# A new pass that orders the queues of a fused attention and gated feed-forward kernel

## The chip, the cores and the metric

The kernel runs on one core of a Trainium2 chip. The core has a matrix engine (TensorE, PE in the rows; its weight loads are PEld), a vector engine (VectorE, DVE), a scalar engine (ScalarE, ACT), a third vector engine (GpSimd, POOL) and a queue that issues transfers (SyncE, SP). The metric is the time of one execution on the device in microseconds (us); smaller is better.

## The reference

The inputs are `q`, `k`, `v` of 8 batches, 8 heads, 576 positions and 64 columns, and three weights. A sliding window of 64 positions bounds the attention, and a gated feed-forward part with a convolution over three neighbouring positions follows:

```python
scores = q @ k^T / 8, kept where 0 <= query - key < 64
attn = softmax(scores)
x = (attn @ v) with the heads side by side          # 8 x 576 x 512
h = maximum(x @ w_in, 0)                            # 8 x 576 x 1024
conv_out = sum of conv_w[k] * h shifted by k - 1    # k = 0, 1, 2
gate = 1 / (1 + exp(-conv_out))
return (h * gate) @ w_out                           # 8 x 576 x 512
```

The weights come to the kernel as words of 64 bits and are turned into 32-bit numbers on the chip.

## The kernel before, in words

The 4608 positions (8 x 576) are cut into NU = 12 units of 384. A unit passes through these steps; the names are those of the functions.

- `qk` (line 330): the scores of one of four parts ("b") of a unit, in two PSUM banks `sc`; in unit 0 two parts use banks `po` instead. `row_max` (337, DVE) adds the mask and takes the largest score of a row, `exps` (347, ACT) the exponentials, `guard` (350), `reciprocal` (353) and `normalise` (358) the division, on DVE in units 0 to 2 and on GpSimd later. In units 0 and 1 `transpose_pe` (364) turns the result round on PE and `untile` (369) copies it to `ub`; later `transpose` (374, DVE) and `place` (386, transfers) do that.
- `values` (441): attention times `v` for one of four groups of columns, in one of two banks `acc`; `split_hi` (445, ACT) and `split_lo` (448, DVE) write it as a high part `xh` and a low part `xl`.
- `mm1` (461): for each of eight blocks f of 128 hidden columns, twelve matmuls in two halves of six, `xh` by `wih`, `xh` by `wil`, `xl` by `wih`, in the same two banks `acc`; `relu` (478, 482) brings the block to `hbuf`. `conv_mid` (488, ACT), `conv_side` (495, DVE, two passes), `sig` (502), `gate` (507), `gate_hi` (511) and `gate_lo` (515) make `gh` and `gl`.
- `mm2` (524): twelve matmuls for each f into four banks `po`, copied to `ot` (555 by ACT, 557 by DVE) and written out (559, 561).

`weights` and `to_f32` (231 to 256) bring in one or two blocks of weights: the transfer (249) lands in `bits`, ACT takes an absolute value (233), GpSimd a maximum (234), DVE shifts (235), joins (237) and adds (241), ACT scales the low words (240), GpSimd casts to the high part (254), DVE subtracts to the low part (255). While this goes on, during the first units, PE fills idle time with matmuls that nobody reads (`keep_busy`, 201), written "fills" below.

What sets the order: every step is put down with `at(t, engine, cost, ...)`: a planned time `t` in units of one block f, an engine, a cost in us, and what it reads and writes. The function `queued` walks through the steps with a clock of its own. For each engine it knows when that engine is free (`free`) and which steps are ready; it takes the one that can start first, and among the ready ones of that engine the smallest `t`. The order in which it takes them is the order of the instructions in each engine's queue; nothing is reordered later. Where the pass sees PE idle between 2 and 110 us of its own clock, it puts in 4 fills per us. The planned times of the lead-in (unit 0, unit 1, weights) and of the later units stand in the table START. PE's costs count 1.75 times before WARM = 34 us of the pass's clock:

```python
end = free[e] = start + turn + x.cost * (1.75 if e == "PE" and start < WARM else 1.0)
```

A group of a unit's steps stands in one call: `moe(u)` puts down `mm1`, `mm2` and what belongs to them, `attend(u + 1, ...)` the values of the next unit, `softmax(u + 2, ...)` the scores of the one after.

Of the kernel before, what the change touches and what calls it, by code (L numbers as in the profile page):

```python
# [8 lines left out]
F32 = mybir.dt.float32  # L9
# [20 lines left out]
BY_PE = 2  # L30
MASKED = -8.0e9
# [17 lines left out]
class Work:  # L49


    def __init__(self, t, eng, cost, do, r, w, kind, mb):
        self.t, self.eng, self.cost, self.do, self.r, self.w, self.kind, self.mb = t, eng, cost, do, r, w, kind, mb
        self.needs, self.after, self.ready = 0, [], 0.0


def queued(works, fill=None):
# [25 lines left out]
    done = 0.0  # L83
# [4 lines left out]
    dma, order, left, now = 0.0, [], len(works), 0.0  # L88
    while left:
        best = None  # L90
        for e, ws in waiting.items():
# [3 lines left out]
            if best is None or start < best[0]:  # L95
# [3 lines left out]
                key=lambda x: x.t - (0.5 if x.kind and x.kind == state[e] else 0.0))  # L99
        waiting[e].remove(x)  # L100
        if fill and e == "PE" and start < FILL_TO:
            t = max(done, FILL_FROM)
            n = int((start - t) * FILL)

            clean = [(end, k) for k, (by, end) in touched.items() if by != "PE" and end < t]
            if n > 0 and clean:
                order.append(Work(x.t, e, 0.0, fill(n, min(clean)[1]), [], [], None, 0))
        if e == "PE":
            done = start + x.cost
# [22 lines left out]
    "v0": -27.718,  # L132
    "pv0": -16.652,
    "conv": -50.105,
    "bits": ((-54.407, -55.57), (-39.376, -39.449)),
    "qk1": -30.664,
    "v1": -7.347,
    "qk2": -0.865,
    "qk0": (-89.392, -49.783, -60.199, -45.186),
    "ex0": (-41.041, -35.906, -29.408, -23.745),  # L140
    "sc1": (-28.59, -27.038, -11.919, -7.749),
    "ex1": (-7.86, -0.101, 0.495, 2.41),
    "mask": -0.464,
    "sig": ((3.579, 6.501, 8.86, 9.928), (2.077, 5.642, 5.863, 10.537), (3.828, 7.108, 8.794, 11.179)),
    "in": (-33.296, -27.752, -22.771, -21.836, -16.12),
    "out": (-13.132, -6.394, 4.658, 7.697),
    "pv": ((4.523, 1.038, 6.096, 5.282), (5.491, 6.42, 7.385, 7.606), (2.552, 5.391, 5.803, 6.224)),
    "ex": ((7.752, 8.302, 8.53, 10.388), (7.962, 8.724, 10.881, 11.654), (5.306, 6.637, 8.454, 9.014)),
}
SWITCH = {"PE": 0.12, "ACT": 1.28}  # L150
WARM = 34.0
# [4 lines left out]
def attention_moe(ctx: ExitStack, tc: tile.TileContext, q, k, v, w_in, conv_w, w_out, out):  # L156
# [50 lines left out]
    def at(t, eng, cost, do, r=(), w=(), kind=None, mb=0):  # L207
        plan.append(Work(t, eng, cost, do, list(r), list(w), kind, mb))


    def load_qk(t, u):

        cut = (0, NX // 2 + W, NX + W), (0, NX // 2, NX)
        for g in range(2):
# [14 lines left out]
    def to_f32(t, n, st, x, kb, kt):  # L229
# [4 lines left out]
        at(t, "POOL", 0.0026 * n + 0.5, lambda: nc.gpsimd.tensor_scalar(x, x, TINY, None, op0=ALU.max), w=kt)  # L234
        at(t, "DVE", 0.00052 * n + 0.25, lambda: nc.vector.tensor_scalar(  # L235
            xu, xu, 3, 0x3FFFFFF8, op0=ALU.logical_shift_left, op1=ALU.bitwise_and), w=kt)
        at(t, "DVE", 0.00104 * n + 0.1, lambda: nc.vector.scalar_tensor_tensor(  # L237
# [3 lines left out]
        at(t, "DVE", 0.00104 * n + 0.1, lambda: nc.vector.tensor_tensor(xu, xu, lw, ALU.add), r=kb, w=kt)  # L241

    def weights(t, src, fs, hi, lo, key, buf, halves):
# [10 lines left out]
        at(t, "POOL", 0.0014 * n + 0.25, lambda: nc.gpsimd.tensor_copy(hi, x), r=kt, w=[f"{key}{f}h" for f in fs])  # L254
        at(t, "DVE", 0.00104 * n + 0.1, lambda: nc.vector.tensor_tensor(lo, x, hi.bitcast(F32), ALU.subtract),  # L255
# [132 lines left out]
    def softmax(u, qk_at, ex_at):  # L388
        for b in range(4):
            g, t = b // 2, qk_at[b]  # L390
            at(t, "PE", 0.70 if wide(u) else 0.62, lambda b=b: qk(u, b), r=[("q", g, b % 2)] + [("k", g, i) for i in range(b % 2 + 1)], w=bank_keys(u, b) + [("turn", b)],
               kind="tiled" if wide(u) else "eight")
            for i in range(NB):
                if block(u, b, i)[1]:
                    at(t + 0.1, "POOL", 0.2, lambda b=b, i=i: nc.gpsimd.memset(ss[b][:, i, :, :W], 0.0), w=[("s", b, i)])
            at(t + 0.17, "DVE", 1.27 if wide(u) else 1.1, lambda b=b: row_max(u, b),
               r=bank_keys(u, b) + (["mask0"] if wide(u) else ["mask1", "mask2"]), w=[("s", b, i) for i in range(NB)] + [("nm", b)])
            t = ex_at[b]
            for i in range(NB):
                at(t, "ACT", 0.78 if wide(u) else 0.74, lambda b=b, i=i: exps(u, b, i), r=[("nm", b)],  # L400
                   w=[("s", b, i), ("sm", b, i)], kind="exp")
            t += 0.45
            sw = [("sm", b, i) for i in range(NB)]
            if u < 3:
                at(t, "POOL", 0.6, lambda b=b: guard(b, nc.gpsimd), w=sw)
            else:
                at(t, "DVE", 0.15, lambda b=b: guard(b, nc.vector), w=sw)
            at(t, "DVE", 0.15, lambda b=b: reciprocal(b), r=sw, w=[("r", b)])
            if u < 3:
# [10 lines left out]
            else:  # L420
                t = max(t, when[-1][2] + 0.1)
                at(t, "DVE", 0.72, lambda b=b: transpose(b), r=sr, w=[("T", g)] + [("bits", i, a) for i in T_BITS[g] for a in range(2)])
                if b % 2:
                    if u == BY_PE:
                        at(t + 0.01, "POOL", 1.0, lambda g=g: zero_blocks(g), w=[("u", g, i) for i in range(4)])
# [161 lines left out]
    for u in range(NU):  # L587
# [5 lines left out]
        for c in range(NC):  # L593
            attend(u + 1, c, pv[c])
# [89 lines left out]
```

## Time and profile before

| | before |
|---|---|
| time, median of 3 runs | 534.14 us (533.28 to 535.07) |
| the profiled execution | 533.38 us |
| its span in the profile | 531.6 us |
| PE busy / weight loads | 523.1 us (98%) / 499.2 us |
| DVE / ACT / GpSimd busy | 381.1 / 405.5 / 115.9 us |
| clock granted to PE | 0.998 of full speed |
| chain that ended last | PE 88%, DVE 10%, ACT 1% |

Busy PE time holds the fills too, so it does not say how much of it is wanted work. A timeline row gives the start, the length and the form of one instruction, or of several alike in a row ("x24"). Matmuls overlap in it: the next one starts before the one before has ended, so the pace of PE is read from start to start. A matmul of `qk`, `values` or a fill is two matrix instructions in the trace (an order that says x12 is x24 there).

### The profile page before, as it was taken

The page shows a single profiled execution, that of the slowest core. Times are in us where ns is not written, and L with a number is a line of the kernel's source. Part 1 is how long each engine was busy: PE and PEld are TensorE (multiplying, and loading weights), DVE is VectorE, ACT ScalarE, POOL GpSimd, SP SyncE. Part 2 cuts the span into 40 slices and gives each one's busy share as a digit, 9 for nine tenths or more (in the row PEclk, how much of TensorE's full clock was granted, in tenths as well). Part 3 has the DMA queues.
Part 4 walks back from the last instruction along what each step waited for, and adds up shares of the span by engine and source line. Part 5 has one row for each costly group of instructions (what it writes and reads, how often), then busy time and mean ns, then how long its engine had stood idle before and what let it go on. Part 6 is the DMA issues. An engine that isn't in the chain of part 4 may idle for free.

```text
span 531.6 us, 14870 instructions
## 1 busy us (share of the span) xinstructions
PE 523.1 (98%) x5802; PEld 499.2 (94%) x5802; DVE 381.1 (72%) x1108; ACT 405.5 (76%) x1034; POOL 115.9 (22%) x208
## 2 busy tenths in 40 slices
PE   9999999999999999999999999999999999999996
PEld 8888889999999999999999999999999999999996
DVE  4899999986677677676686776776776865864552
ACT  5889886799888788689689679779769769653541
POOL 6556663203121121112012022022022011100000
PEclk9999999999999999999999999999999999999999
DMA  8883760166472282273173164254155133110011
GB/s 286 318 300 123 263 224 20 27 181 211 125 249 55 76 252 65 76 236 85 48 241 106 42 222 132 47 198 156 46 185 170 46 121 105 46 61 0 1 60 61
DMA packets 29318, 69.98 MB, mean 132 GB/s; under 512 B 5696, under 2 KB 17472, under 8 KB 29248
## 3 DMA queue, kind: packets, MB, share of 16 engines
q1 hardware_dynamic: 29248, 69.03, 40.5%
q8 instruction: 46, 0.75, 0.6%
q14 instruction: 24, 0.20, 0.1%
HBM read 47.73 MB, written 9.47 MB: 108 GB/s over the span
## 4 chain that ended last, share of the span: by engine, by line
PE 88%; DVE 10%; ACT 1%; issue 1%; POOL 0%
PE po L524 38%; PE acc L461 35%; PE acc L441 6%; PE sc L330 6%; PE acc L201 2%; DVE w L241 1%; DVE c L495 1%; DVE s L337 1%; DVE w L237 1%; DVE wil L255 1%; DVE s L358 1%; DVE w L235 1%; DVE xl L448 1%; ACT ub L369 0%; ACT s L347 0%
## 5 line engine op out<-in xcount | busy, mean ns | idle before, releaser
L524 PE MATMUL po<-gh,woh 128*128 128x386 f32 (+1 forms) x384 | 133.1, 347 | 0.0
L461 PE MATMUL acc<-xh,wih 128*128 128x384 f32 x384 | 131.9, 344 | 1.1 <-DVE xl L448 0.9
L461 PE MATMUL acc<-xh,wil 128*128 128x384 f32 x384 | 129.8, 338 | 0.4 <-DVE wil L255 0.4
L524 PE MATMUL po<-gl,woh 128*128 128x386 f32 (+1 forms) x384 | 130.1, 339 | 0.0
L461 PE MATMUL acc<-xl,wih 128*128 128x384 f32 x384 | 129.7, 338 | 0.0
L524 PE MATMUL po<-gh,wol 128*128 128x386 f32 (+1 forms) x384 | 129.7, 338 | 0.0
L495 DVE SCALAR_TENSOR_TENSOR c<-hbuf,cw,c 128x386 f32<-128x386 f32 (+1 forms) x192 | 110.8, 628 | 19.9 <-ACT c L488 19.0
L347 ACT ACTIVATE s<-s,nm 128x96 f32<-128x96 f32 (+2 forms) x288 | 105.6, 371 | 9.7 <-DVE nm L337 9.3
L358 POOL TENSOR_TENSOR s<-s,r 128x576 f32<-128x576 f32 x36 | 45.7, 1271 | 196.4 <-DVE r L353 196.4
L524 PEld LDWEIGHTS po<-gh,woh 128*128 128x128 f32 x384 | 72.3, 188 | 4.3
L461 PEld LDWEIGHTS acc<-xh,wih 128*128 128x128 f32 x384 | 72.1, 188 | 4.2 <-DVE xl L448 1.6
L461 PEld LDWEIGHTS acc<-xh,wil 128*128 128x128 f32 x384 | 72.2, 188 | 0.7 <-DVE wil L255 0.7
L524 PEld LDWEIGHTS po<-gl,woh 128*128 128x128 f32 x384 | 72.4, 188 | 0.0
L524 PEld LDWEIGHTS po<-gh,wol 128*128 128x128 f32 x384 | 72.4, 188 | 0.0
L461 PEld LDWEIGHTS acc<-xl,wih 128*128 128x128 f32 x384 | 72.1, 188 | 0.0
L337 DVE CUSTOM_DVE_ANT_0 s<-sc,mask 128x96 f32<-128x96 f32 (+2 forms) x276 | 53.2, 254 | 21.3 <-PE sc L330 20.5
L515 DVE TENSOR_TENSOR gl<-c,gh 128x772 fp32r<-128x772 f32 (+1 forms) x48 | 52.8, 1099 | 20.1 <-ACT gh L511 19.5
L502 ACT ACTIVATE c<-c 128x772 f32<-128x772 f32 (+1 forms) x48 | 40.8, 850 | 33.8 <-DVE c L495 33.5
L482 ACT ACTIVATE hbuf<-acc 128x384 f32<-128x384 f32 x64 | 30.6, 487 | 34.7 <-PE acc L461 34.1
L347 ACT ACTIVATION_READ_ACCUMULATOR s<-s,nm 128x1 f32 x288 | 55.1, 191 | 0.0
L488 ACT ACTIVATE c<-hbuf,cw 128x386 f32<-128x386 f32 (+1 forms) x96 | 53.7, 610 | 0.1
L507 DVE TENSOR_TENSOR c<-c,hbuf 128x772 f32<-128x772 f32 (+1 forms) x48 | 45.2, 942 | 9.2 <-ACT c L502 9.2
(64 smaller groups left out, 641.8 us busy)
## 6 DMA issues: line engine op xcount, KB each, us to landing
v<-in_v_dram SPq DMA_DIRECT2D x24, 768.0 KB, 4.7
ub<-T SPq DMA_DIRECT2D x240, 48.0 KB, 2.0
k<-in_k_dram SPq DMA_DIRECT2D x22, 448.0 KB, 5.3
q<-in_q_dram SPq DMA_DIRECT2D x22, 384.0 KB, 6.2
out_dram<-T SPq DMA_DIRECT2D x8, 772.0 KB, 3.5
T<-in_w_in_dram SPq DMA_DIRECT2D x8, 512.0 KB, 5.4
T<-in_w_out_dram SPq DMA_DIRECT2D x8, 512.0 KB, 4.3
out_dram<-T SPq DMA_DIRECT2D x3, 768.0 KB, 6.1
```

Source lines behind the costliest of these rows:

```text
L330: nc.tensor.matmul(banks_of(u, b)[h][r:r + rows, i * P + o:i * P + n], qs[hs, 2 * g + p, t:t + rows], ks[hs, 2 * g + p, t + o:t + n], star ...
L337: nc.vector.tensor_tensor_reduce(out=ss[b][:, i, h, o:n], in0=banks_of(u, b)[h][:, i * P + o:i * P + n], in1=mask[m][:, o:n], scale=-0.125 ...
L347: nc.scalar.activation(x, x, AF.Exp, bias=nms[b][:, e], scale=-1.0, accum_out=sms[b][:, e])
L358: on.tensor_tensor(sv, sv, rs[b].unsqueeze(2).broadcast_to([P, 2 * NB, n]), ALU.mult)
L441: nc.tensor.matmul(acc[bank(("v", u, c))][h * D:(h + 1) * D, t * W:(t + 1) * W], vs[:, c, t, h], ub[g][:, 2 * p:2 * p + 2, 2 * t + h], sta ...
L461: nc.tensor.matmul(acc[bank(("m", u, f))][:, :NX], w[:, f, c], x[u % 2][:, c], start=(c == 0 and j == 0), stop=(c == NC - 1 and j == 2))
L488: nc.scalar.activation(cs[i % 2][:, a, :n], hbuf[:, f, 1:1 + n], AF.Copy, scale=cw[:, 1, f:f + 1])
L495: nc.vector.scalar_tensor_tensor(c, hbuf[:, f, e:e + n], cw[:, e, f:f + 1], c, op0=ALU.mult, op1=ALU.add)
L502: nc.scalar.activation(c, c, AF.Sigmoid)
L507: nc.vector.tensor_tensor(c, c, hbuf[:, 2 * i:2 * i + 2, 1:1 + n], ALU.mult)
L515: nc.vector.tensor_tensor(gls[ring(u, i)][:, :, :n], cs[i % 2][:, :, :n], ghs[ring(u, i)][:, :, :n].bitcast(F32), ALU.subtract)
L524: nc.tensor.matmul(po[o][:, :n], w[:, f, es], x, start=(f == 0 and j == 0), stop=(f == NF - 1 and j == 2))
```

## The change

- The pass `queued` gets a sixth argument of a step, `port`: how long it holds what DVE and GpSimd cannot use at once. A step of DVE that has it starts no earlier than the last such step of GpSimd ends in the pass's clock, and the other way round. `two(...)` puts down a step that holds it for its whole cost (tensor operations on DVE with operands in SBUF, the cast and the normalisation on GpSimd); GpSimd's maximum holds it for PORT_CL = 0.5 us only.
- Several costs are set anew (line by line in the diff), WARM goes from 34 to 5, and the whole table START is new. Among it: the first two weight transfers change places, and the times of `values`, `exps` and `sig` in the later units move.
- The scores of part n of unit u + 2 are put down beside the values of column group n, by `scores`, one part at a time; the load of `q` and `k` follows after every second part.
- The copy of the last bank of the last unit is cut in two halves of 193 columns, one on ACT and one on DVE, each with its own transfer.
- LATE, CATCH and CAST_ACT and the argument `early` stand at values with which they change nothing.

```diff
+        if x.port:
+            if e == "POOL" and start < port["DVE"]:
+                free[e] = port["DVE"]
+                continue
+            start = max(start, port["POOL"])
+            port[e] = start + x.port
...
-            t = max(done, FILL_FROM)
+            t = max(free[e], FILL_FROM)
...
-    "bits": ((-54.407, -55.57), (-39.376, -39.449)),
+    "bits": ((-51.706, -50.713), (-31.489, -48.442)),
...
-    "pv": ((4.523, 1.038, 6.096, 5.282), (5.491, 6.42, 7.385, 7.606), (2.552, 5.391, 5.803, 6.224)),
+    "pv": ((4.247, 1.621, 6.62, 5.614), (4.827, 3.03, 5.128, 5.557), (4.971, 4.767, 5.829, 5.368)),
...
-WARM = 34.0
+PORT_CL = 0.5
+WARM = 5.0
...
-        at(t, "POOL", 0.0026 * n + 0.5, lambda: nc.gpsimd.tensor_scalar(x, x, TINY, None, op0=ALU.max), w=kt)
+            at(t, "POOL", 0.0027 * n + 0.02, lambda: nc.gpsimd.tensor_scalar(x, x, TINY, None, op0=ALU.max), w=kt, port=PORT_CL)
...
+            if u == LAST and o == NC - 1:
+                for eng, cost, cut, copy in (("ACT", 0.3, slice(0, w // 2), nc.scalar.copy), ("DVE", 0.3, slice(w // 2, w), nc.vector.tensor_copy)):
+                    at(t + 0.05 * o, eng, cost, lambda cut=cut, copy=copy: copy(ot[:, NC - 1, cut], po[NC - 1][:, cut]), r=[("po", o)], w=[("ot", o, cut.start)])
+                    at(t + 0.05 * o + 0.01, "SP", 0.7, lambda cut=cut: nc.sync.dma_start(out[u, :, NC - 1, cut], ot[:, NC - 1, cut]), r=[("ot", o, cut.start)], mb=0.1)
+                continue
...
+    coming = [(u, b) for u in range(2, NU) for b in range(4)]
...
+        for n, (x, y) in enumerate(zip(pv, START["ex"][min(u, 2)])):
+            if u > 0 or n >= LATE:
+                scores(x + 0.005, n0 + y, n)
```

The numbers of all instructions of each kind stay as they are, but for 102 fills in the place of 93, the extra half copy, its transfer, and 42 loads of ACT's function tables in the place of 58.

Two places show how the queues move. The first is PE's queue in a later unit (values of two groups, then scores; `acc_110` and `acc_111` are the two banks, `ub_61` and `ub_62` the two halves of a unit's attention, 12 matmuls a group, 24 to a part of the scores, all but the first two of which are left out). Before:

```order
1409 L441 MATMUL acc_111<-ub_61,v 64x64 x12
1410 L441 MATMUL acc_110<-ub_62,v 64x64 x12
1411 L330 MATMUL sc_108<-k,q 32x96
1412 L330 MATMUL sc_109<-k,q 32x96
...
1485 L461 MATMUL acc_111<-xl_65,wih 128x384
1486 L441 MATMUL acc_110<-ub_62,v 64x64 x12
1487 L330 MATMUL sc_108<-k,q 32x96
1488 L330 MATMUL sc_109<-k,q 32x96
...
1511 L524 MATMUL po_113<-gh_99,woh 128x386
```

And now:

```order
1404 L479 MATMUL acc_111<-xl_65,wih 128x384
1405 L349 MATMUL sc_108<-k,q 32x96
1406 L349 MATMUL sc_109<-k,q 32x96
...
1429 L459 MATMUL acc_110<-ub_62,v 64x64 x12
1430 L459 MATMUL acc_111<-ub_62,v 64x64 x12
1431 L349 MATMUL sc_108<-k,q 32x96
1432 L349 MATMUL sc_109<-k,q 32x96
...
1455 L542 MATMUL po_113<-gh_99,woh 128x386
```

The four groups of values of a unit stood in three places, one pair and two alone; now they stand in two pairs, the second of them directly between two parts of scores.

The second place is the start of ACT's queue (`s_80` to `s_82` are parts 0 to 2 of unit 0's scores, `w_105` the first two blocks of `w_in`). Before:

```order
2 L347 ACTIVATE s_80,sm_88<-s_80,nm_84 128x64 x2
3 L347 ACTIVATE s_80,sm_88<-s_80,nm_84 128x128 x4
4 L347 ACTIVATE s_81,sm_89<-s_81,nm_85 128x128 x6
5 L233 ACTIVATE w_105<-T 128x512
6 L347 ACTIVATE s_82,sm_90<-s_82,nm_86 128x64 x2
```

And now:

```order
2 L366 ACTIVATE s_80,sm_88<-s_80,nm_84 128x64 x2
3 L366 ACTIVATE s_80,sm_88<-s_80,nm_84 128x128 x2
4 L246 ACTIVATE w_105<-T 128x512
5 L366 ACTIVATE s_80,sm_88<-s_80,nm_84 128x128 x2
6 L246 ACTIVATE w_105<-T 128x512
7 L366 ACTIVATE s_81,sm_89<-s_81,nm_85 128x128 x6
```

The first block of weights now stands ahead of the last exponentials of part 0, and the second ahead of those of part 1.

## Rows read from the trace of the kernel before

**Rows 1.** Windows: length, busy us (instructions) of PE, PEld, DVE, ACT, POOL; clock; DMA

```profile
0.00:34.47 34.47, 32.51 (x433) 29.39 (x433) 24.57 (x100) 25.96 (x96) 22.06 (x62) 1.00 0.87 308
34.47:75.13 40.66, 38.26 (x496) 34.95 (x497) 40.62 (x115) 35.11 (x97) 22.78 (x18) 1.00 0.59 195
110.00:527.44 417.44, 417.44 (x4552) 401.07 (x4550) 280.66 (x825) 318.22 (x794) 58.79 (x112) 1.00 0.37 115
```

**Rows 2.** The same view of the fills alone (line 201): length, PE, PEld

```profile
0.00:34.47 34.47, 22.20 (x138) 19.27 (x138) 1.00 0.87 308
34.47:75.13 40.66, 4.68 (x38) 4.66 (x38) 1.00 0.59 195
```

**Rows 3.** Waits of PE, whole span: us in total, times, longest

```profile
PE acc L441 <- DVE xl L448: 1.1, 1, 1.1
...
PE acc L461 <- DVE xl L448: 0.9, 2, 0.5
PE acc L441 <- DMA v<-in_v_dram: 0.8, 1, 0.8
PE acc L461 <- DVE wil L255: 0.4, 1, 0.4
PE acc L461 <- POOL w L234: 0.2, 1, 0.2
```

**Rows 4.** Timeline of PE in a later unit: start, length, instruction

```profile
347.77 1.62 PE L441 MATMUL acc<-ub,v 128*64 128x64 f32 x48
349.32 0.83 PE L330 MATMUL sc<-k,q 64*32 64x96 f32 x48
...
355.76 0.34 PE L461 MATMUL acc<-xl,wih 128*128 128x384 f32 x1
356.02 0.92 PE L441 MATMUL acc<-ub,v 128*64 128x64 f32 x24
356.87 0.83 PE L330 MATMUL sc<-k,q 64*32 64x96 f32 x48
357.64 0.45 PE L524 MATMUL po<-gh,woh 128*128 128x386 f32 x1
357.92 0.34 PE L524 MATMUL po<-gh,wol 128*128 128x386 f32 x1
```

**Rows 5.** Chain that ended last: the last run of matmuls

```profile
514.79 12.66 PE po L524 x72
```

**Rows 6.** Timeline of PE: eight fills and the matmul behind them

```profile
39.68 1.93 PE L201 MATMUL po<-spare 128*128 128x112 f32 x16
41.59 0.42 PE L461 MATMUL acc<-xh,wih 128*128 128x384 f32 x1
```

**Rows 7.** Timelines of GpSimd and DVE: operations that overlap

```profile
40.10 2.78 POOL L234 TENSOR_SCALAR w<-w 128x1024 f32<-128x1024 f32 x1 [2.21 <-ACT w L233]
...
40.28 1.67 DVE L358 TENSOR_TENSOR s<-s,r 128x768 f32<-128x768 f32 x1
41.87 1.21 DVE L241 CUSTOM_DVE_ANT_0 w<-T,w 128x2048 uint16<-128x2048 uint16 x1
```

**Rows 8.** Lead-in: transfer issued at 4.80 (us to landing), ACT, DVE

```profile
T<-in_w_in_dram SPq DMA_DIRECT2D x1, 512.0 KB, 6.0
...
8.82 0.38 ACT L347 ACTIVATE s<-s,nm 128x128 f32<-128x128 f32 x1
...
12.86 0.96 DVE L358 TENSOR_TENSOR s<-s,r 128x768 f32<-128x768 f32 x1
```

**Rows 9.** Timeline of DVE in a later unit: conv_side pair, end of a row_max

```profile
351.24 1.15 DVE L495 SCALAR_TENSOR_TENSOR c<-hbuf,cw,c 128x386 f32<-128x386 f32 x2
...
358.82 0.08 DVE L337 DVE_READ_ACCUMULATOR2_ANT nm<- 128x1 f32 x1
```

**Rows 10.** The end: DVE's last copy, the last four transfers on SP

```profile
527.47 0.56 DVE L557 COPY T<-po 128x386 f32<-128x386 f32 x1 [0.49 <-PE po L524]
...
526.41 1.98 SPq L559 DMA_DIRECT2D out_dram<-T  x4
```

More of the change, by code (lines that the diff above doesn't have):

```diff
@@ L30 @@
 BY_PE = 2
+LATE = 0
+CATCH = 99
+CAST_ACT = 99
 MASKED = -8.0e9
@@ L87, in queued @@
             waiting[x.eng].append(x)
-    dma, order, left, now = 0.0, [], len(works), 0.0
+    dma, port, order, left = 0.0, {"DVE": 0.0, "POOL": 0.0}, [], len(works)
     while left:
@@ L106, in queued @@
             if n > 0 and clean:
-                order.append(Work(x.t, e, 0.0, fill(n, min(clean)[1]), [], [], None, 0))
-        if e == "PE":
-            done = start + x.cost
+                order.append(Work(x.t, e, 0.0, fill(n, min(clean)[1]), [], [], None, 0, 0.0))
         turn = SWITCH[e] if e in SWITCH and (x.kind != state[e] if e == "PE" else x.kind and x.kind != state[e]) else 0.0
@@ L205, in attention_moe, with at, two, load_qk @@
     plan = []
-    def at(t, eng, cost, do, r=(), w=(), kind=None, mb=0):
-        plan.append(Work(t, eng, cost, do, list(r), list(w), kind, mb))
-    def load_qk(t, u):
+    def at(t, eng, cost, do, r=(), w=(), kind=None, mb=0, port=0.0):
+        plan.append(Work(t, eng, cost, do, list(r), list(w), kind, mb, port))
+    def two(t, eng, cost, do, **kw):
+        at(t, eng, cost, do, port=cost, **kw)
+    def load_qk(t, u, gs=(0, 1)):
         cut = (0, NX // 2 + W, NX + W), (0, NX // 2, NX)
-        for g in range(2):
+        for g in gs:
             c = slice(2 * g, 2 * g + 2)
@@ L253, in weights @@
         to_f32(t, n, st, x, kb, kt)
-        at(t, "POOL", 0.0014 * n + 0.25, lambda: nc.gpsimd.tensor_copy(hi, x), r=kt, w=[f"{key}{f}h" for f in fs])
-        at(t, "DVE", 0.00104 * n + 0.1, lambda: nc.vector.tensor_tensor(lo, x, hi.bitcast(F32), ALU.subtract),
+        if key == "out" and fs[0] >= CAST_ACT:
+            at(t, "ACT", 0.0009 * n + 0.2, lambda: nc.scalar.copy(hi, x), r=kt, w=[f"{key}{f}h" for f in fs])
+        else:
+            two(t, "POOL", 0.00127 * n, lambda: nc.gpsimd.tensor_copy(hi, x), r=kt, w=[f"{key}{f}h" for f in fs])
+        two(t, "DVE", 0.00104 * n + 0.07, lambda: nc.vector.tensor_tensor(lo, x, hi.bitcast(F32), ALU.subtract),
            r=kt + [f"{key}{f}h" for f in fs], w=[f"{key}{f}l" for f in fs])
@@ L584, in attention_moe, with scores @@
     load_v(START["v1"], 1)
-    softmax(1, START["sc1"], START["ex1"])
+    for b in range(4):
+        softmax(1, b, START["sc1"][b], START["ex1"][b], b)
+    coming = [(u, b) for u in range(2, NU) for b in range(4)]
+    def scores(t, t_ex, k):
+        if coming:
+            u, b = coming.pop(0)
+            softmax(u, b, t, t_ex, k)
+            if b % 2 and u + 1 < NU:
+                load_qk(max(t + 0.1, NF * (u - 2) + 7.8), u + 1, (b // 2,))
     for u in range(NU):
```

139 lines of the change are left out of this document (71 added, 68 removed).

## The prediction

> **What bounds the kernel now.** I read the windows first [rows 1]. From 110.00 to 527.44 us PE is busy for the whole 417.44 us, and the clock stands at 1.00, its upper level (2.4 GHz), while DVE has 280.66 and ACT 318.22 us of work there. So from 110 us on nothing but PE's own queue sets the time, and a faster DVE or ACT is worth nothing unless PE waits for it. Before that the picture is another one: from 34.47 to 75.13 us DVE is busy for 40.62 of 40.66 us and PE for 38.26. In PE's 38.26 us lie 4.68 us of fills, and in the 32.51 us of the first stretch 22.20 us [rows 2]. The list of PE's waits comes next [rows 3]: 1.1, 0.9, 0.8, 0.4 and 0.2 us, 3.4 us in all, nearly all on results of DVE and one on the load of `v`, and none of them after 75 us. (A further 1.0 us at the very start is the wait for the memory of the fills to be set, which the change leaves.) So the span is a sum: wanted PE work, fills, 3.4 us of waits, and some 4 us behind the last matmul. The change leaves the number of wanted matmuls alone; it can save time by making them cheaper to string together, by fewer fills, by fewer waits, or at the end.
>
> **Part 1, the order in the later units.** The start-to-start times of PE [rows 4] give a price to each change of the kind of work. A group of values alone runs from 356.02 to 356.87, 0.85 us; a pair of groups from 347.77 to 349.32, 1.55 us. Joining two groups saves 2 x 0.85 - 1.55 = 0.15 us. By the order, the values stood in 38 places and now stand in 27: 11 x 0.15 = 1.65 us less. Next, the pace of unbroken matmuls is 12.66 us for 72, 0.176 us each [rows 5]. The last one ahead of the values takes 355.76 to 356.02, 0.26 us, and the first one behind the scores 357.64 to 357.92, 0.28 us: 0.085 and 0.105 us too much. `mm1` and `mm2` were left for scores, values or transposes at 44 places and entered again at 45; now it is 33 and 35. That is 11 x 0.085 + 10 x 0.105 = 2.0 us less. Against this, scores are now followed directly by values in 8 later units, which the trace before does not show. It costs between nothing and what the way from matmuls to values costs, 0.085 us, so 0 to 0.7 us for the eight; I take 0.3, the middle, as neither end has a row of this kind. All of it lies on PE's own queue, with no other work to hide it. Sum: -1.65 - 2.0 + 0.3 = -3.35 us.
>
> **Part 2, the fills.** Eight fills run from 39.68 to 41.59 us, 0.24 us each [rows 6]. There are 102 for 93: 9 x 0.24 = 2.2 us more. They are instructions in PE's queue and run whether PE would have had to wait or not, so they are a cost that stays even if everything else arrives early. (64 instead of 69 stand ahead of the first `mm1`, 38 instead of 24 behind it.)
>
> **Part 3, the waits of the lead-in.** The 3.4 us [rows 3] go, and new ones come, since the queues of all engines are new up to about 110 us. Why the waits should get fewer: the pass of before knows nothing of DVE and GpSimd hindering each other, and the trace shows them doing it. The normalisation of DVE takes 0.96 us when GpSimd rests [rows 8] and 1.67 us beside the start of GpSimd's maximum [rows 7]. Such delays make DVE's results later than planned, so that PE, whose fills were counted by the plan, stands and waits behind them. The new pass counts 0.5 us of hindrance for a maximum, close to the 0.71 us seen. The new waits have a lower end at zero. As the value I take 0.8 us for the load (the port has nothing to do with it) and 0.7 us of the 2.4 us that are put down to DVE: 1.5 us. The upper end I take at the double of before, 6.8 us, because ACT and DVE get a new order too (below).
>
> At this place a rule speaks against the change. The rows say that the hindrance ends early: the add of DVE at 41.87 reads two tensors in SBUF, lies inside GpSimd's maximum of 2.78 us, and takes 1.21 us, while the one that met its first part lost 0.71 us [rows 7]. The Trainium skill ("SBUF — State Buffer", its part on the two physical sides) says that whoever of the two starts first holds the shared ports for its whole instruction and the other blocks fully. This trace does not agree for the maximum: 1.21 us is not 2.78. By the Trainium skill the pass, with its 0.5 us, would overlook some 2.3 us for each of nine maxima.
>
> **Part 4, the end.** The last copy, 0.56 us on DVE [rows 10], becomes two halves side by side, which saves 0.2 us or so; but SP issues five transfers instead of four behind each other, at 1.98 / 4 = 0.5 us each, and the second half's transfer queues behind the first half's. The transfer itself is smaller. Bounds: 0.25 us less to 0.4 us more; I take 0, between two nearly equal ends.
>
> **Part 5, what is hidden.** 16 fewer loads of function tables and the shorter counts of ACT and DVE come at no gain: after 110 us both have over 90 us to spare [rows 1]. That cover is also what a later `relu` or `split_lo` would fall back on; if it were gone, PE would stand at the next `mm1`.
>
> **The sum.** -3.35 (order) + 2.2 (fills) - 3.4 + 1.5 (waits) + 0 (end) = -3.05 us. Against the profiled execution (533.38 us, of which 531.6 are the span) that is a span of 528.55 us. The median of the runs is 534.14 us, 0.76 above the profiled one; taken from the median: 531.1 us. Without any wait of PE it would be 529.6 us, and the joins and the end at their good bounds give 529.0.
>
> **The rivals.**
> *The plan comes out no better than the old one.* In unit 0 the first block of weights now stands in ACT's queue ahead of the last exponentials. Its transfer is issued at 4.80 and lands 6.0 us later, at 10.8 us, and ACT has done the four exponentials ahead of it at 8.8 us [rows 8], so ACT would sit for about 2 us with the exponentials of parts 0 and 1 queued behind it, and GpSimd's and DVE's share in the weights now stands ahead of the first normalisation, which was at 12.86 us. The values of unit 0 then come some us later, `mm1` waits behind them. For it: DVE has no time to catch up [rows 1]. Against it: PE runs 64 fills there and has nothing wanted to do, so that a delay of that part is paid for by fills first. With waits as long as before (3.4 us) the gain is 1.15 us, 533.0 us; with the double, 536.4 less the fills' cover, so about 534 to 536. Chance 0.26 for a time within 0.3%, 533.0 us as its middle.
>
> *A wait in every later unit, slower.* Between two parts of scores there now stands in eight units only a pair of values, 1.55 us. The banks `sc` have to be emptied by `row_max` in that time. After scores that end at 357.64 us the last row maximum ends at 358.90, 1.26 us later [rows 4, 9], when DVE comes to them at once: 0.3 us to spare. If DVE is in a `conv_side` pair instead, which takes 1.15 us [rows 9], PE waits 0.85 us with all later matmuls queued behind it, eight times: 6.8 us, 531.1 + 6.8 = 537.9 us. It decides from (3.05 + 1.6) / 8 = 0.58 us a unit on. Against it: by the new order nothing but `row_max` stands in DVE's queue between the two parts at that place. Chance 0.08.
>
> *The port held throughout.* If a maximum did hold DVE off for its whole 2.78 us where the pass counts 0.5, nine of them put DVE 20 us behind its plan in the stretch where it is full, and PE with it, less what fills cover: some 540 to 550 us. The rows speak against it, as said. Chance 0.02. (The rule of the Trainium skill that is told in part 3 would have it so.)
>
> **How the numbers follow.** Two times of this kernel can be told apart from about 0.3%, 1.6 us. The forecast, 531.1 us, faster, has 0.64; the no-better plan 0.26; the waits in the later units and the held port, slower, 0.10 together. The forecast is faster than 532.5 as long as the new waits of PE stay under 2.95 us. The range: at the low end no wait at all with the good bounds, 529.0, and 0.2 for the spread of the runs, 528.8; at the high end the no-better plan with 5.4 us of waits, 535.0. Outside stay the slower rivals (0.10) and some 0.08 of better and worse ends.
>
> **What would show it.** Right: from 110 us to the last matmul PE again busy without a gap, with a unit shorter by about 0.35 us (eight units of one pair joined and one way out of the matmuls less: 0.15 + 0.19); 204 fill instructions; PE's list of waits under 2 us. Wrong in part 1: pairs of values that take more than 1.55 us, or scores to values with a gap. Wrong in part 3: PE waiting for `xl`, `wil` or `gl` before 75 us in sum by more than 3.4 us. The second rival shows as waits of the scores' weight loads on DVE line 356, the first as ACT idle near 9 to 11 us and a first `mm1` later than 34.47 us.

## The result and the profile after

The changed kernel takes 538.38 us (median of 14 runs, 535.69 to 541.02), the kernel before 534.12 (14 runs, 533.09 to 535.07): ratio 1.0081, 95% interval 1.0062 to 1.0099. It is slower by 4.3 us where 3.0 us less were forecast. The profiled execution took 536.78 us, its span is 534.9.

First the windows, cut at the first `mm1`, as in [rows 1], with the stretch from 75.13 to 110 us added. Columns: length, busy us (instructions) of PE, PEld, DVE, ACT, POOL; granted clock, share of the transfer engines, GB/s.

```profile
0.00:33.33 33.33, 30.00 (x422) 27.35 (x422) 23.14 (x98) 24.32 (x87) 22.57 (x61) 1.00 0.85 312
33.33:75.13 41.80, 38.01 (x511) 34.92 (x508) 41.28 (x105) 34.55 (x94) 24.00 (x21) 1.00 0.56 193
75.13:110.00 34.87, 34.38 (x333) 32.87 (x322) 33.62 (x82) 28.73 (x65) 11.42 (x14) 1.00 0.29 82
110.00:530.39 420.39, 418.91 (x4575) 405.19 (x4573) 276.54 (x825) 299.56 (x775) 61.01 (x114) 1.00 0.37 114
```

From 110 us on PE is no longer busy without a gap: 418.91 of 420.39 us. The list of PE's waits (us in total, times, longest), which answers [rows 3]:

```profile
PE po L383 <- DVE s L377: 2.2, 3, 1.1
PE sc L349 <- issue: 1.4, 1, 1.4
PE acc L459 <- DVE xl L466: 1.4, 2, 1.1
...
PE sc L349 <- DVE s L377: 0.7, 1, 0.7
PE po L349 <- DMA q<-in_q_dram: 0.5, 1, 0.5
PE acc L479 <- ACT hbuf L500: 0.4, 1, 0.4
PE acc L459 <- DMA ub<-T: 0.4, 1, 0.4
PE acc L479 <- DVE xl L466: 0.4, 1, 0.4
PE acc L459 <- ACT hbuf L500: 0.4, 1, 0.4
```

The second row is new in kind: 1.4 us in the middle of one part's scores, from 436.17 to 437.58 us, for which the profile names nobody ("issue"). The others (the row left out is the 1.0 us at the very start) all lie before 110 us and make 6.4 us, where the 3.4 us of before were to become 1.5. ACT's queue in the lead-in shows what the first rival described (compare [rows 8]):

```profile
8.22 0.19 ACT L366 ACTIVATION_READ_ACCUMULATOR s<-s,nm 128x1 f32 x1
10.86 0.68 ACT L246 ACTIVATE w<-T 128x512 f32<-128x512 f32 x1 [2.45 <-DMA T<-in_w_in_dram]
...
15.90 0.96 DVE L377 TENSOR_TENSOR s<-s,r 128x768 f32<-128x768 f32 x1
```

Busy PE time holds fills, so I use a second measure, **the lag**: the time t less the wanted matmuls started by then, each at its unbroken pace (0.176 us for one of `mm1` or `mm2`, 0.70 for a group of values, 0.71 or 0.76 for a part of scores, 0.11 for a transpose). All of them make some 480 us in every kernel here (479.4 is taken off in the table), so a kernel is as much slower as its lag grows more. From the starts of all matmuls, us:

| lag at | 35 | 50 | 70 | 110 | last matmul | from 110 on |
|---|---|---|---|---|---|---|
| before | 23.6 | 27.2 | 32.1 | 35.3 | 47.7 | 12.4 |
| after | 22.9 | 29.8 | 36.6 | 39.4 | 51.0 | 11.7 |
| h2 (new lead-in, old later order) | 22.9 | 29.3 | 35.5 | 37.0 | 49.8 | 12.9 |
| d1 (after, no later loads) | 22.9 | 29.8 | 36.2 | 39.0 | 48.5 | 9.5 |
| h3v (old lead-in, new order from the third unit, `v` late) | 23.6 | 27.2 | 32.2 | 35.5 | 44.8 | 9.3 |

The changed kernel loses 4.1 us against before by 110 us and gets 0.7 back later, one stall of 1.4 us paid. At 35 us it is still ahead; the loss is made between 35 and 70 us. The last three rows belong to the experiments.

### The profile page after: what moved, and what is told of

The parts are those of the page before. It is cut to its first block, busy times and chain, and to the rows that moved or that the text cites. A ratio compares the mean times of both kernels' runs of the same rounds, so it can differ in the third digit from the quotient of the medians.

```text
span 534.9 us, 14870 instructions
## 1 busy us (share of the span) xinstructions
PE 521.6 (98%) x5820; PEld 500.3 (94%) x5820; DVE 374.9 (70%) x1108; ACT 387.8 (72%) x1019; POOL 119.0 (22%) x208
## 4 chain that ended last, share of the span: by engine, by line
PE 81%; DVE 11%; DMA 3%; SPq 2%; issue 2%; ACT 1%; POOL 0%; ACTq 0%; DVEq 0%; POOLq 0%
PE po L542 37%; PE acc L479 33%; PE acc L459 6%; PE sc L349 5%; DMA T<-in_w_in_dram 2%; DVE c L513 2%; DVE s L356 1%; SPq L405 1%; DVE w L253 1%; DVE w L257 1%; DVE s L377 1%; DVE w L251 1%; SPq L232 1%; DVE wil L274 1%; ACT s L366 1%
## 5 line engine op out<-in xcount | busy, mean ns | idle before, releaser
L513 DVE SCALAR_TENSOR_TENSOR c<-hbuf,cw,c 128x386 f32<-128x386 f32 (+1 forms) x192 | 109.5, 623 | 26.6 <-ACT c L506 26.6
L377 POOL TENSOR_TENSOR s<-s,r 128x576 f32<-128x576 f32 x36 | 42.5, 1182 | 217.3 <-DVE r L372 217.3
L525 DVE TENSOR_TENSOR c<-c,hbuf 128x772 f32<-128x772 f32 (+1 forms) x48 | 49.0, 1035 | 10.9 <-ACT c L520 10.9
L533 DVE TENSOR_TENSOR gl<-c,gh 128x772 fp32r<-128x772 f32 (+1 forms) x48 | 45.1, 954 | 13.6 <-ACT gh L529 13.0
```

What stands on the lines that cost most here:

```text
L377: on.tensor_tensor(sv, sv, rs[b].unsqueeze(2).broadcast_to([P, 2 * NB, n]), ALU.mult)
L513: nc.vector.scalar_tensor_tensor(c, hbuf[:, f, e:e + n], cw[:, e, f:f + 1], c, op0=ALU.mult, op1=ALU.add)
L525: nc.vector.tensor_tensor(c, c, hbuf[:, 2 * i:2 * i + 2, 1:1 + n], ALU.mult)
L533: nc.vector.tensor_tensor(gls[ring(u, i)][:, :, :n], cs[i % 2][:, :, :n], ghs[ring(u, i)][:, :, :n].bitcast(F32), ALU.subtract)
```

## The experiments

"Before" in a ratio is always the kernel before, run on the same chip between the others.

**The two halves of the change, apart.** My first theory put the loss into the lead-in. `h1_later_only` and `h2_leadin_only` share out the table START; by their order `h1` is the kernel before up to the first unit and the changed one from the second on.

```diff
 h1, on the kernel before (sig and ex alike); h2 does the reverse on the changed kernel
-    "pv": (..., (5.491, 6.42, 7.385, 7.606), (2.552, 5.391, 5.803, 6.224)),
+    "pv": (..., (4.827, 3.03, 5.128, 5.557), (4.971, 4.767, 5.829, 5.368)),
```

> The kernel before with only the new times of the later units (second and third rows of pv, ex and sig); pass, costs, lead-in and last copy as before. The order of all engines is then that of before up to the first unit and that of after from the second unit on. Theory L (the loss of 4.3 us sits wholly in the lead-in, and the later units gain what the lag curves of the two traces show between 110 and 420 us, 2.2 us): 531.9 us, 531.0 to 532.7, one group of runs at clock 1.00. Rival S (the later order brings its own stall, such as the 1.4 us in the middle of one unit's scores at 436 us of after's trace, and pays part of it back): 533.0 to 535. Rival P (the planner's own times hold: it puts the last matmul of this kernel at 526.1 us against 522.6 for before): 537.

> The changed kernel with the old times of the later units: the new pass, costs, lead-in and last copy, the old order from the second unit on. Theory L: the loss without the gain, 538.4 + 2.2 = 540.6 us, 539.5 to 542, and the runs still in two groups by granted clock (1.000 and 0.995 to 0.997), if that too comes with the lead-in. Rival S: 536 to 538.5, as the loss would be partly the later order's. Under S the low granted clock may be gone.

> The kernel before with the new times of the later units and the last copy in halves by two engines. Theory: the halves change nothing measurable (the page of after shows 4.18 us from the last matmul to the end against 4.16 before), so the time of h1_later_only within 0.3 us. Rival: the halves give the 0.25 us that half of a 0.56 us copy saves.

> The changed kernel unchanged, on the chip of this call: 538.4 us, its runs in two groups, one at clock 1.000 and 535.7 to 537, one at 0.995 to 0.997 and 538 to 541. If the two groups belong to the chip of the first measurement and not to the kernel, one group here, 536.5. The profile, if it falls in the lower group, shows where the granted clock is below 1.0: theory L expects a place between 10 and 75 us, where TensorE waits longest; rival: in the later units.

Measured: `h1` 538.06 us (ratio 1.0079, 1.0057 to 1.0101), `h2` 535.83 (1.0032, 1.0020 to 1.0044), `h1s` 539.61 (1.0106, 1.0088 to 1.0125), `a0` 538.31 (1.0080, 1.0062 to 1.0099). Theory L fell: the half that was to gain costs as much as the whole change, and the lead-in by itself only 1.7 us. But `h1` does not show the later units alone. Its lag grows by 7.0 us between 70 and 110 us, that of before by 3.2: with the new second rows behind the old lead-in, 38 fill instructions stand in one place, from 87.44 to 91.83 us, and a wait of 0.5 us behind them. The fills alone, from 70 to 110 us (length, busy PE, PEld; clock; DMA):

```profile
70.00:110.00 40.00, 4.39 (x38) 4.38 (x38) 1.00 0.28 90
```

Its one stall is 1.2 us. The third rows by themselves come below (`h3`). `a0` shows two stalls of the nameless kind:

```profile
PE sc L349 <- issue: 4.0, 2, 2.4
```

All four traces with the new later order have one or two (1.2 to 2.4 us); those of before and of `h2` have none.

**What the stalls are.** The trace holds every packet of the transfer engines. On a queue of its own (q8, kind "instruction") 46 packets of 16,384 bytes come in during a run, one for each 256 instructions of PE; the page of before has them too (queue and kind: packets, MB, share of the 16 engines):

```profile
q8 instruction: 46, 0.75, 0.6%
```

Counting PE's recorded instructions (weight loads too) and taking off 256 for each earlier packet gives a **place**: where no data moves, the next packet starts when PE passes place 155. In `a0`, from 110 us on, it starts 0 to 1.8 us after that where little or no data moves, and 2 to 5 us after it where a load of `q`, `k`, `v` or a store of `out` fills the engines. Each nameless stall of over 0.4 us from 110 us on, twelve in seven traces, begins exactly at place 449, and ends 1.2 to 1.6 us after the missing packet has landed. The latest landing in a trace without stalls was at place 404. Lateness alone is no stall: the trace of before has packets up to 4.4 us late, that of `h3v` (below), until the last matmul, up to 5.1. It takes a late packet where PE is fast. A part of scores is 96 instructions of PE in 0.76 us, a pair of values 96 in 1.55 us, twelve matmuls of `mm1` 24 in 2.1 us: where scores, values and scores stand in a row, PE eats its blocks fastest. I call this theory F (late blocks). `d1` takes the traffic away, `b1` is its control, `d2` moves one load:

```diff
 d1 on the changed kernel, b1 on the kernel before (v alike)
-    ... nc.sync.dma_start(sb[:, c, e], dram[u, :, c, e])
+    ... u < 3 and nc.sync.dma_start(sb[:, c, e], dram[u, :, c, e])
 d2 on the changed kernel, in load_v
-        for g in range(2):
+        for g in (0, 1) if u < 3 else (1, 0):
...
-            at(t, "SP", 0.7, ..., w=[("v", g)], mb=0.79)
+            at(t, "SP", 0.7, ..., r=[("v", 1)] if g == 0 and u > 2 else [], w=[("v", g)], mb=0.79)
```

> The changed kernel with the loads of q, k and v left out from the fourth unit on (the buffers keep the third unit's data), every other instruction and all orders as in the changed kernel. Theory F: TensorE's instructions come in blocks of 256 through the same 16 transfer engines as the data; in the traces so far a block starts to move 0 to 1.2 us after TensorE passes place 155 of the block before where no data is moving, and 3 to 5 us after where a load of q, k, v or a store of out is; TensorE stands still when it reaches place 449 first (it did in four of four traces with the new later order, 1.2 to 2.4 us each time, never in the two with the old one, whose highest places are 364 and 380). Without the loads the blocks come early and no trace shows place 449 or an idle stretch of over 0.9 us after 110 us; the time falls by the stalls, 1.4 to 4.0 us a run: 535.3 us, 534.5 to 536.3. Rival D (the dense stretches of scores and values stall by themselves, or the stall is the granted clock's): 537.5 to 539, and place 449 is still met.

> The kernel before with the same loads of q, k and v left out from the fourth unit on; the control. Theory F: its blocks are never late, so nothing is gained: 534.1 us, 533.3 to 534.5. Rival D2 (the loads slow something else in every unit, a port or the stores): both kernels gain alike, 532 to 533.

> The changed kernel with one move on SyncE's queue, from the fourth unit on: the load of v's first half goes behind that of its second half, so that it no longer starts together with the store of the last unit's output just ahead of the dense stretch; the other engines' orders are the same, row for row. Theory F: the largest delay of a block, 4.8 and 5.2 us in the trace of the second profile of the changed kernel, is that of out and v together (1.6 MB); with the store alone it is about 2 us, the two stalls go, and the time is 535.5 us, 534.8 to 536.8. Rival D: no change, 538.3. A third case: the loads, now closer together, meet the next block instead, 537 to 539, with place 449 at another block.

Measured: `d1` 534.13 us (0.9990, 0.9979 to 1.0002), `b1` 533.10 (0.9980, 0.9963 to 0.9997), `d2` 534.29 (0.9996, 0.9984 to 1.0009). Moving one of SyncE's loads in each unit behind another, with the four other queues row for row the same, takes 0.85% off, 4.5 us. (The trace of `d2` has a granted clock of 0.56 from 6.8 us on, so its rows are not used; that of `h3v`, below, shows the same move.) In `d1` PE has no gap from 110 us on, and the latest block lands at place 372:

```profile
110.00:527.86 417.86, 417.86 (x4573) 404.54 (x4571) 274.91 (x824) 299.64 (x774) 60.54 (x114) 1.00 0.17 48
```

`b1` gains 0.2%, so the loads cost before little. `bv` asks the same of `d2`'s move:

```diff
 the edit of d2 on the kernel before
```

> The kernel before with the load of v's first half behind that of its second from the fourth unit on, all other engines' orders unchanged. Theory F: its blocks of instructions land by place 364 at the latest, so the move has no stall to take away: 533.9 to 534.2, the time of before; at most the 1 us that it gained with no later loads at all. Rival: the move gains 3 us or more here too, and then late blocks are not what it cures.

Measured: 533.92 us (0.9984, 0.9967 to 1.0001). The interval reaches from 1.8 us less to nothing: the move is worth 4.5 us only where late blocks stop PE.

**Where the granted clock falls.** The changed kernel's times spread over 5 us, with a mean granted clock of 0.995 to 0.997 in 8 of 14 runs; these took 538.1 to 541.0 us, the six at 1.000 took 535.7 to 537.0. Two more executions:

```diff
 c1: the changed kernel, c2: h3_third_rows (below), unchanged
```

> The changed kernel once more, for one look. Eight of its fourteen first executions had a mean granted clock of 0.995 to 0.997 and took 2 to 3 us longer; d1 and d2, which have no late blocks, show 0.998 to 1.000. If this execution is one of the slow ones, theory: TensorE stands still at place 449 for 1.5 us or more and the granted clock falls from 1.0 to 0.5 behind that, for 3 to 5 us. Rival: the clock falls in the lead-in, before 75 us, where TensorE waits most.

> The kernel of h3_third_rows once more, for one look at the same question; eight of its twelve executions had 0.995 to 0.997. Theory: the clock falls behind a stall at place 449 in the later units; rival: in the lead-in.

Both executions were of that kind (538.40 and 537.88 us). PE's timeline in `c1`, from a part of scores on:

```profile
432.73 0.83 PE L349 MATMUL sc<-k,q 64*32 64x96 f32 x48
433.52 1.62 PE L459 MATMUL acc<-ub,v 128*64 128x64 f32 x48
435.07 0.76 PE L349 MATMUL sc<-k,q 64*32 64x96 f32 x41
437.65 0.36 PE L349 MATMUL sc<-k,q 64*32 64x96 f32 x7 [1.82 <-issue]
...
440.00 0.53 PE L479 MATMUL acc<-xh,wih 128*128 128x384 f32 x1
440.32 0.52 PE L479 MATMUL acc<-xh,wil 128*128 128x384 f32 x1
...
442.77 0.34 PE L479 MATMUL acc<-xh,wih 128*128 128x384 f32 x1
442.95 0.34 PE L479 MATMUL acc<-xh,wil 128*128 128x384 f32 x1
```

PE runs out of instructions after 41 of 48 matmuls. The transfers from 431.2 us, when PE passed place 155, to 435.2 us, just ahead of the packet (queue and kind: packets, MB, share of the 16 engines), and the same to 436.3 us:

```profile
q1 hardware_dynamic: 429, 1.19, 98.1%
...
q1 hardware_dynamic: 457, 1.30, 89.2%
q8 instruction: 1, 0.02, 1.2%
```

For 4 us data take 98.1% of the engines and no instruction comes through. Behind the stall the pace is 0.32 us from start to start instead of 0.176: the clock records have 0.5 (1.2 GHz) from 439.2 to 442.6 us. `c2` has the same: a stall of 1.87 us at 190.0, clock 0.5 from 192.6 for 3.4 us. So each of these two pays twice, 1.8 us and some 1.5 more (3.4 us at 0.32 instead of 0.176). `a0` stood still for 2.4 us and kept clock 1.00, so a stall does not always bring it; why it does at times is open. By the two groups of times, some 2.5 of the 4.5 us are lost at the full clock too, by the stalls themselves, and the rest comes with the lower clock (an estimate; the slower executions may also have longer stalls).

By the Trainium skill ("Runtime: NRT & Kernel Launch", "Instruction fetch mechanics") instructions come in blocks of 16 KiB, 256 of them, by a queue of the sequencer's own, and crossing a block is mostly hidden. The packets agree; "hidden" holds in the trace of before, and not here.

**The order without the stalls.** `h3` takes only the third rows of pv, ex and sig into the kernel before, `h3v` adds the move of `d2`, `h5v` puts the old second rows into `d2`.

```diff
 h3, on the kernel before (sig and ex alike)
-    "pv": (..., (5.491, 6.42, 7.385, 7.606), (2.552, 5.391, 5.803, 6.224)),
+    "pv": (..., (5.491, 6.42, 7.385, 7.606), (4.971, 4.767, 5.829, 5.368)),
 h5v, on d2
-    "pv": (..., (4.827, 3.03, 5.128, 5.557), (4.971, 4.767, 5.829, 5.368)),
+    "pv": (..., (5.491, 6.42, 7.385, 7.606), (4.971, 4.767, 5.829, 5.368)),
```

> The kernel before with only the third rows of pv, ex and sig (third unit on) from the changed kernel; the lead-in and the first two units stay as before. Theory F: the later order is worth 3.0 us (lag of TensorE from 110 us to the end: 12.5 us in the trace of before, 9.5 in that of the changed kernel without its later loads), of which the third rows have some 2.7, and pays 1.2 to 4 us back in late blocks of instructions, as every trace of the changed kernel with its loads did: 531.5 + 1.2 to 4 = 533 to 535.5, likeliest 533.8, with place 449 met in the trace. Rival: no stalls when the lead-in is the old one: 531.5.

> The same with the load of v's first half behind that of its second, as in d2_v_late. Theory F: gain without the stalls: 531.5 us, 530.8 to 532.3, faster than both kernels; no place 449. Rival (the move of the load was worth 4 us in d2_v_late for a reason of that kernel's own): as h3_third_rows, 533 to 535.

> The changed kernel with the second rows of pv, ex and sig (the second unit) taken from before and the load of v's first half behind that of its second, as in d2_v_late: new lead-in, old second unit, new order from the third. Theory: of the 3.7 us that TensorE has lost by 110 us in the changed kernel, the second rows have 1.4 to 2 (lag at 110 us 39.0 to 39.4 in the changed kernel, 37.0 with both later rows old), so 534.3 - 1.7 = 532.6 us, 531.8 to 533.3. Rival (the loss is the lead-in's alone and the second rows only moved it): 534.3, 533.7 to 535.

Measured: `h3` 535.40 us (1.0028, 1.0010 to 1.0046), `h3v` 530.37 (0.9941, 0.9918 to 0.9965), `h5v` 533.40 (0.9975, 0.9960 to 0.9991). The trace of `h3` has three stalls, that of `h3v` none:

```profile
PE sc L330 <- issue: 2.6, 3, 1.2
```

PE's matmuls are the same in both, one by one. Laid side by side, `h3` falls behind by 1.0, 0.7 and 1.5 us at just these three places, 3.2 of the 3.3 us by which the two spans differ (531.6 and 528.3 us). So the same order is slower or faster than before by where one load of each unit stands (in the trace of `h3` 5 to 6 us earlier). `h3v` beats both kernels; from 110 us on PE has no gap and the lag grows by 9.3 us instead of 12.4:

```profile
110.00:524.18 414.18, 414.18 (x4552) 400.88 (x4551) 274.40 (x825) 299.44 (x778) 58.52 (x112) 1.00 0.37 116
```

**The lead-in.** Three kernels take suspects away: the first two transfers of `w_in`; these, the last two and the second two of `w_out`; all fills.

```diff
 h2n1 and h2n3 on h2 (shortened; both set the first buffer to zero by DVE), f1 on d2
+                if key == "in" and f < 2: return                                               # h2n1
+                if key == "in" and (f < 2 or f > 5) or key == "out" and f in (2, 3): return     # h2n3
-FILL, FILL_FROM, FILL_TO = 4.0, 2.0, 110.0
+FILL, FILL_FROM, FILL_TO = 0.0, 2.0, 110.0                                                      # f1
```

> The kernel of h2_leadin_only (new pass and lead-in, old later order) with the first two transfers of w_in left out; their buffer is zeroed at the start by VectorE instead. All other orders are the same. Theory A (ScalarE's first absolute value, ahead of the last exponentials of the first part, waits for the transfer and is on the path): ScalarE's idle 2.2 to 2.6 us at 8.2 to 8.4 us goes, the first normalise moves from 15.4 to 15.9 us to about 13, and the lead-in's loss against before, 1.6 us, falls by 1 to 2.4: 533.4 to 534.8, likeliest 534.2. Rival: the path behind it is set by something else (q and k of the next unit, the fills, DVE), and the time stays at 535.8, 535.3 to 536.3.

> The kernel of h2_leadin_only with three groups of transfers left out: the first two of w_in (buffer zeroed), the last two of w_in and the second two of w_out (buffer keeps old data); all other orders the same. Theory B (the lead-in loses because ScalarE's queue stands behind weights that have not landed; the chain of the trace runs through the last w_in transfer from 30.3 to 35.7 us): 533.5 us, 532.5 to 534.5, the lag of TensorE at 70 us 33 to 34 instead of 35.5. Rival (VectorE, which the chain names from 39 to 65 us without a break, sets the path, and the time before is made up there): 535.4, 535 to 536, lag at 70 us over 35.

> The kernel of d2_v_late without any of the 204 fill matmuls. Theory (fills only take time in which TensorE would wait, since their number comes from the planned wait): 534.3 us less 0 to 1. Rival 1 (my term of +2.2 us for nine more fill matmuls a planned wait too long): 532.5 to 533.3. Rival 2 (without them TensorE's clock is granted at its lower level somewhere in the lead-in): 536 or more, with a granted clock below 1.00 in the windows up to 75 us.

Measured: `h2n1` 535.44 us (1.0018, 1.0006 to 1.0029), `h2n3` 534.58 (1.0011, 0.9997 to 1.0025), `f1` 534.51 (1.0007, 0.9991 to 1.0023). Theory A fell: with ACT's wait gone the lag at 70 us is 35.7, against 35.5. Theory B has by the ratios 1.1 of the 1.7 us, with an interval that overlaps that of `h2`, and its lag at 70 us (35.4) did not fall as expected. `f1` shows what stands behind the fills: without them PE waits, and the rows name for whom (waits of PE, and two windows):

```profile
PE sc L349 <- DMA q<-in_q_dram: 8.6, 2, 4.4
PE po L383 <- DVE s L377: 4.4, 4, 1.9
PE acc L479 <- ACT hbuf L500: 3.2, 2, 2.5
...
20.00:30.00 10.00, 7.81 (x94) 6.42 (x92) 9.76 (x28) 9.81 (x35) 6.72 (x6) 0.67 0.86 330
50.00:60.00 10.00, 10.00 (x111) 9.59 (x112) 9.72 (x24) 7.26 (x12) 8.06 (x7) 0.74 0.33 110
```

The second of the two 4 us waits for `q` ends at 15.4 us: it is the first part of unit 1's scores, which now stands ahead of unit 0's transposes in PE's queue and needs its own load. In the other traces of this lead-in 48 fill instructions cover it. The third row is `mm1` at 49.75 us, behind ACT's queue. The granted clock falls to 0.67 and 0.74 of full speed without the fills, and the time is the same as `d2`'s. So what PE does in the lead-in waits, for the most part, for DVE, ACT and loads at either level; but no run takes the fills away at an unchanged clock, and a small cost of fills could hide behind what the lower clock takes.

The lag says where the lead-in loses: `h2` is 0.7 us ahead of before at 35 us, and 3.4 behind at 70. Fills alone, from 35 to 50 us, before and `h2`:

```profile
35.00:50.00 15.00, 1.93 (x16) 1.93 (x16) 1.00 0.58 196
35.00:50.00 15.00, 4.55 (x38) 4.18 (x36) 1.00 0.54 183
```

2.6 us more are fills, idle time that the plan itself foresaw, while DVE is busy for 14.97 of the 15 us in `h2`. DVE, which the new pass was to relieve, is no less busy: up to 110 us for 100.3 us in `h2` and 99.8 in before. No run shows that the wait for the weights at 8.2 us or that for `q` at 15.4 us reaches that far.

**The last copy and the shared port.** `s1` is the kernel before with the halves alone, `m1` a row of short groups behind the kernel's end.

```diff
 s1, on the kernel before: the new lines "if u == LAST and o == NC - 1" of the change
 m1, behind the kernel before: 128x1024 tiles, each group started by an ACT operation
+        for group in ((add, add), (shift, shift), (pmax,), (pcopy,), (pmult,), (pmax, add, add, add), ...
```

> The kernel before with its last copy and store in halves by ScalarE and VectorE, nothing else. Theory: 0, from 0.25 us less to 0.4 more: what stands from the last matmul's start to the end of the span stays near 4.5 us. Rival (h1s_later_split was 1.5 us slower than h1_later_only because of it): 535.5.

> The kernel before, and behind its last store ten short groups on spare tiles of 128x1024, each started by one operation of ScalarE: VectorE's add and its shift alone, GpSimd's maximum, copy and product alone, and then GpSimd's maximum, copy or product beside three adds, and the maximum or copy beside three shifts. Theory of the new pass (GpSimd and VectorE exclude each other for an operation's whole length, the maximum for its first 0.5 us only): beside the copy and the product the first add begins only when GpSimd has ended, 1.3 us or 2.0 and more later, or GpSimd is longer by the adds; beside the maximum an add is later by 0.5 us. Rival (they share, and each is slowed): adds at 1.2 us grow in length beside each of them. Third case: nothing moves, adds at 1.1 to 1.2 us beside each.

Measured: `s1` 534.60 us (1.0003, 0.9984 to 1.0023). In the trace of after the halves do not run side by side; ACT's waits for DVE's:

```profile
530.76 0.36 DVE L574 COPY T<-po 128x193 f32<-128x193 f32 x1 [0.49 <-PE po L542]
531.15 0.32 ACT L574 COPY T<-po 128x193 f32<-128x193 f32 x1 [0.43 <-DVE T L574]
```

`m1` ran once, for the rows: adds alone, the maximum and the product of GpSimd alone, then each beside three adds (L620 add, L626 maximum, L632 product):

```profile
528.33 2.48 DVE L620 TENSOR_TENSOR k<-w 128x1024 f32<-128x1024 f32 x2 [0.39 <-ACT w L617]
534.66 2.77 POOL L626 TENSOR_SCALAR w<-w 128x1024 f32<-128x1024 f32 x1 [48.09 <-ACT w L617]
540.79 1.89 POOL L632 TENSOR_TENSOR w<-w 128x1024 f32<-128x1024 f32 x1 [1.18 <-ACT w L617]
543.81 4.46 DVE L620 TENSOR_TENSOR k<-w 128x1024 f32<-128x1024 f32 x3 [10.39 <-ACT w L617]
543.86 3.80 POOL L626 TENSOR_SCALAR w<-w 128x1024 f32<-128x1024 f32 x1 [1.18 <-ACT w L617]
...
555.09 5.32 DVE L620 TENSOR_TENSOR k<-w 128x1024 f32<-128x1024 f32 x3 [1.18 <-ACT w L617]
555.14 2.92 POOL L632 TENSOR_TENSOR w<-w 128x1024 f32<-128x1024 f32 x1 [3.57 <-ACT w L617]
```

Three adds alone would be 3.72 us. GpSimd, which starts second, is longer by 1.03 us in both cases, most of the 1.2 us that were left of the first add; of the adds only the second is longer: by 0.72 us beside the maximum, by 1.57 beside the product. (The groups with the copy and with shifts, not shown, have the same form.) So they do exclude each other, one holder after the other; the product holds for most of its 1.89 us, the maximum for 0.72 of its 2.77. By the Trainium skill ("SBUF — State Buffer", on the two physical sides) the holder blocks the other for its whole instruction: for DVE's adds and nearly for the product this agrees, for the maximum not. The pass's premise was sound; its 0.5 us for a maximum are 0.22 short.

## Why the prediction was wrong

In per cent of before: new lead-in +0.32 (`h2`), new order from the third unit without late blocks -0.59 (`h3v`), new second rows +0.21 (`d2` less `h5v`), late blocks +0.85 (the changed kernel less `d2`). Together +0.79 where +0.81 was measured: +1.7, -3.1, +1.1 and +4.5 us. The second term comes from the old lead-in; on the new one (`h2` to `h5v`) it is -0.57. The third is the weakest: the intervals of `d2` and `h5v` overlap, and the lag of `h5v` at 110 us, 38.8, is hardly below the 39.0 of `d1`.

- **Part 1, -3.35 us, was right as far as it went.** `h3v` shows -3.1 us of lag from 110 us on. Pairs of values take 1.55 us; values behind scores cost about 0.03 us more than the pace of scores, close to the 0.3 us that I took for eight places.
- **The step that failed stands ahead of it**, in "nothing but PE's own queue sets the time": the instructions of that queue have to come in, too, through engines that carry the data. The term is missing from the sum, +4.5 us. I priced joined groups as pure gain, and with scores on both sides they are what uses up the blocks fastest. No row of before showed a stall, since its latest block lands at place 364; but the instruction packets were in that trace, and what the Trainium skill says of instruction fetch (named above) could have been weighed. The second rival had the place, the scores between two parts in the later units, and a wrong cause: in the changed kernel's trace `row_max` makes PE wait nowhere.
- **Part 2, +2.2 us for fills, was mis-sized.** Up to 110 us the fills take 28.3 us in before and 28.5 in the changed kernel, 0.2 us more: five fewer run ahead of the first `mm1`, where 69 took 22.2 us, 0.32 each and not 0.24. With no fills at all the time is that of `d2` within 0.2%, so they stand mostly in waits that are there anyway; nor are they a cost "that stays even if everything else arrives early", as their number follows the planned wait.
- **Part 3, -1.9 us net, has the wrong sign.** Together with the fills I had +0.3 us for the lead-in; `h2` has +1.7, and by the times some 1.1 more go to the second rows. I assumed 1.5 us of new waits from old ones; they are 6.4 us, +3.0 net. The sign that I had set, `xl`, `wil` and `gl` over 3.4 us, did not come (1.8 us): PE waits for the normalised attention instead, 2.9 us, which the old list does not have. My row for hindrance that ends early was misread, too: the add at 41.87 us ends at 43.08, behind the maximum (42.88), and so does not lie inside it; that a maximum holds DVE off for a part only rests on `m1`. The first rival saw ACT's idle 2.45 us rightly and is still not the cause (`h2n1`); the first `mm1` came earlier than before (33.33 us), not later. `q` of unit 1 ahead of the transposes would hold PE to 15.4 us anyway; that this load is on the path is read from rows, not tried, and at 35 us nothing is lost yet. What makes the lead-in's 1.7 us between 35 and 70 us is open; between single executions its lag at 70 us differs by up to 1 us.
- **Part 4, 0, was right** in its size (`s1`) and wrong in its picture: the halves follow each other (DVE from 530.76 to 531.12 us, ACT from 531.15).

## What to carry to other kernels

Where one queue is busy without a gap, ask what feeds it: count its instructions in the densest stretch, and look which transfers fill the engines just then. When short instructions are drawn together, keep large loads and stores away from that place; moving one load of each unit by 5 to 6 us gave 4.5 us here, more than the new order itself. And a plan that gains in one part should be tried in halves, since the gain and the loss of this one were in different rows of a table.

## What the runs showed of the hardware

- PE's instructions arrive in packets of 16,384 bytes behind queued data: from 110 us on up to 5.2 us late in `a0` and `c1`, with up to 1.6 MB moved in between. PE stands still at place 449, and goes on 1.2 to 1.6 us after the packet has landed.
- In the trace of after, 15 of SyncE's 349 issues take 0.9 to 1.9 us where most take 0.33 to 0.6, and all 15 overlap in time with one of the 46 instruction packets of PE (in before 16 of 17); two of them, at 30.43 and 49.06 us (1.48 and 1.46 us), lie in the lead-in beside packets at 30.1 and 48.8 us.
- Behind two of the stalls (1.82 and 1.87 us) the granted clock was 0.5 for 3.4 us; a longer one (2.38 us) left it at 1.00.
